# Channel-major down-projection with stationary weights in a GFNet and MLP-mixer kernel: residual on VectorE, 32x32 block transposes, 256-byte stores

## The chip, the core and the metric

The kernel runs on one core of a Trainium2 chip. The time is that of one execution on the device in microseconds (us). TensorE (PE in the profile) multiplies matrices and writes its sums to PSUM banks; PEld is its weight load. VectorE (DVE) and ScalarE (ACT) read PSUM and write SBUF. GpSimd (POOL), SyncE (SP) and ScalarE issue DMAs. Every engine takes its own instructions in program order and waits on semaphores for the others.

## The reference: what is computed

The batch is 8, a sequence has 3008 tokens, a token has 256 channels. All results are float32; the four mixer weights arrive as float64.

```python
X = np.fft.rfft(x, axis=1)                       # x: (8, 3008, 256)
Y = X * (filt_r + 1j * filt_i)[None, :, :]
y = np.fft.irfft(Y, n=3008, axis=1)
...
h = np.maximum(y.transpose(0, 2, 1) @ w_tok1, 0.0) @ w_tok2     # token mixing, 3008 -> 256 -> 3008
u = y + h.transpose(0, 2, 1)
h2 = np.maximum(u @ w_ch1, 0.0) @ w_ch2                         # channel mixing, 256 -> 1536 -> 256
return u + h2
```

## The kernel before

**The filter.** A sequence of 3008 is taken as 64 x 47 points. `a_unit` does the 64-point transforms on TensorE, ScalarE copies them out and stores them to `z_tmp` in HBM. `b_unit` (L344) loads them again, does the 47-point transform and multiplies by the filter in six VectorE instructions (L352 to L357) from the one PSUM bank `b`; `bi_unit` (L360) does the inverse 47-point transform of the product one step later, and ScalarE copies it to SBUF (L366) and stores it to `g_tmp`. The inverse 64-point transform is never done by itself: its matrix `wai` is folded into the token weights (`w1_fold`) and applied again in `u_unit` (L416).

**The mixer.** `mix(b)` handles one sequence. `token_hidden` makes the token hidden layer in 96 matmul instructions (L397). After it the sequence goes by in `MT` = 6 token tiles `m` of 512 tokens, the last of 448. For a tile, `u_unit` writes `ut`, which is u with channels on the partitions: two halves `dh` of 128 channels by 512 tokens. Then there are `JT` = 12 steps `jt` of 128 hidden channels each. `hidden` (L420) has weights `wc1` as the stationary operand and `ut` moving, two matmuls, and ScalarE applies the relu (L426). `down` (L429) comes two steps later and has the hidden activations `hh` as the stationary operand, 128 tokens at a time, and `wc2` (256 columns) moving: four matmuls a step, one for each quarter q of the tile. So the output has tokens on the partitions, in the two banks `po0` and `po1`. In step `jt` = 0 eight matmuls against an identity matrix (L441) first put `ut`, transposed, into the same banks: that is the residual u. The profile counts two matmul instructions and two weight loads for each float32 matmul in the code. After step 11 ScalarE copies `po0` and VectorE `po1` to SBUF (L452 to L455), and GpSimd stores them in four DMAs (L459), each row run 2 KB long (two neighbouring tokens).

**The order of the work** is written out by hand, as the program order of every engine. In step i of `mix` come, in this order: a piece of weight conversion from float64 (`convert`, only at the start of sequence 0); `hidden` of item i; `u_unit` for the next tile at `jt` 5 and 7; one step of the filter of the next group of sequences, given after the `yield`; `down` of item i-2. A tile's last `down` so stands in step 12m + 13 of its sequence. The groups are (0), (1, 2), (3, 4), (5, 6), (7): during sequence 0 a filter step comes in every step i, in sequences 1 to 6 in every step with even i, and in sequence 7 there is none. A group's filter takes 24 steps of `a_unit` for each of its sequences, two empty ones, and 33 of `b_unit` and `bi_unit`.

**Buffers.** The banks `po0`, `po1`, `b`, `i`, `acc` and `a` exist once each, `pg` (of `hidden`) twice. The tile `u` has two buffers, `hh` four, the output tile `o` two. The conversion of the weights (`rounded`, L204 to L212) is one ScalarE and five VectorE instructions per chunk; the chunks of `wc1` and `wc2` that are not needed at once are converted in steps 0 to 9 of sequence 0 (`LAST`).

Of the kernel before, what the change touches and what calls it, by code (L numbers as in the profile page):

```python
# [10 lines left out]
FP32 = mybir.dt.float32  # L11
# [3 lines left out]
ALU = mybir.AluOpType  # L15
# [4 lines left out]
N1 = 47  # L20
N2 = 64
NF = N // 2 + 1
D = 256
P = 128
K2 = 32
A = 24
KR = 4 * A
HALF = 64
# [7 lines left out]
DC = 1536  # L36
JT = DC // P
DH = D // P
MT = 6
NG = 8  # L40
AHEAD = 6
# [3 lines left out]
def _make_tables():  # L45

    n2 = np.arange(N2)
    wa = np.zeros((P, P))
    wai = np.zeros((P, P))
    for h in range(2):
        r = slice(h * 64, h * 64 + 64)
        for k2 in range(K2):
            th = 2 * np.pi * ((n2 * k2) % N2) / N2  # L60
            c, s = np.cos(th), np.sin(th)
            re, im = 4 * k2 + 2 * h, 4 * k2 + 2 * h + 1
            wa[r, re] = c
# [12 lines left out]
    wi = np.zeros((P, K2, KR))  # L76
    for k2 in range(K2):
        for s in range(2 * A):
            if s < A:
                k, sign, q = k2 + 64 * s, 1.0, s  # L80
            else:
                j = s - A + 1
                k, sign, q = 64 * j - (k2 if k2 else 32), -1.0, 32 + s - A
                if j == A and k2:
                    continue
            th = 2 * np.pi * ((n1 * k) % N) / N
            c, sn = np.cos(th), np.sin(th)
            edge = k in (0, NF - 1)
            if edge:
                sn = np.zeros(N1)  # L90
            if k2:
                wb[re, k2, q] = c
                wb[im, k2, q] = sign * sn
                wb[re, k2, HALF + q] = -sn
                wb[im, k2, HALF + q] = sign * c
            else:
                src = re if s < A else im
                wb[src, k2, q] = c
                wb[src, k2, HALF + q] = -sn
                m = 1.0 if edge else 2.0  # L100
                wi[q, k2, src] = m * c
                wi[HALF + q, k2, src] = -m * sn
    wi[:, 1:, :] = wb[:, 1:, :].transpose(2, 1, 0)
    wi /= N
    f = np.float32
    return wa.astype(f), wai.astype(f), wb.astype(f), wi.astype(f), np.eye(P, dtype=f)


@with_exitstack
def kernel(  # L110
# [10 lines left out]
):  # L121
    nc = tc.nc

    wa_np, wai_np, wb_np, wi_np, id_np = _make_tables()
    wa_d = nc.inline_tensor(wa_np, name="wa_t").ap()
    wai_d = nc.inline_tensor(wai_np, name="wai_t").ap()
    wait_d = nc.inline_tensor(np.ascontiguousarray(wai_np.T), name="wait_t").ap()
    wb_d = nc.inline_tensor(wb_np, name="wb_t").ap()
    wi_d = nc.inline_tensor(wi_np, name="wi_t").ap()
    id_d = nc.inline_tensor(id_np, name="id_t").ap()  # L130


    z_d = nc.dram_tensor("z_tmp", (B, K2, KR, D), FP32, kind="Internal").ap()
# [2 lines left out]
    def pool(name, bufs, **kw):  # L136
        return ctx.enter_context(tc.tile_pool(name=name, bufs=bufs, **kw))

    glob = pool("glob", 1)
# [8 lines left out]
    h1p = pool("h1p", 1)  # L148
    up = pool("up", 2)
    hp = pool("hp", 4)  # L150
    op = pool("op", 2)
    psum = pool("psum", 1, space=bass.MemoryType.PSUM)
    psg = pool("psg", 2, space=bass.MemoryType.PSUM)

    def bank(tag):
        return (psg if tag == "pg" else psum).tile([P, 512], FP32, tag=tag, name="ps_" + tag)

    xlast = glob.tile([P, XC, D], FP32, name="xlast")
    wa = glob.tile([P, P], FP32, name="wa")
    wai = glob.tile([P, P], FP32, name="wai")  # L160
    wai_t = glob.tile([P, P], FP32, name="wai_t")
    ident = glob.tile([P, P], FP32, name="ident")
    filt = glob.tile([P, K2, D], FP32, name="filt")
    w1 = glob.tile([P, A, DT], FP32, name="w1")
    w2 = glob.tile([P, TC, N], FP32, name="w2")
# [1 line left out]
    wc2 = glob.tile([P, JT, D], FP32, name="wc2")  # L167
# [86 lines left out]
    def wc1_load(i):  # L254
        c, q = divmod(i, DC // 512)
        st = stage(512)
        nc.gpsimd.dma_start(st, moe_w_ch1[ts(c, P), ts(q, 512)])
        yield
        rounded(st, 512, [(lambda v: v, wc1[:, c, ts(q, 512)])])

    def wc2_load(i):
        st = stage(512)
        nc.gpsimd.dma_start(st.rearrange("p (j d) -> p j d", d=D),
                            moe_w_ch2[ts(i, 2 * P), :].rearrange("(j p) d -> p j d", p=P))
        yield
        rounded(st, 512, [(lambda v: v, wc2[:, 2 * i:2 * i + 2, :].rearrange("p j d -> p (j d)"))])


    LAST = ((wc2_load, 0), (wc1_load, 1), (wc1_load, 4), (wc2_load, 1), (wc1_load, 2), (wc2_load, 2), (wc1_load, 5),
# [50 lines left out]
    def dft(bs):  # L320
# [10 lines left out]
        wbs, wis, t2s, t3s, prods = {}, {}, {}, {}, {}  # L331
# [28 lines left out]
        def bi_unit(k):  # L360
            ps = bank("i").rearrange("p (b d) -> p b d", b=2)[:, 0:nb, :]
            nc.tensor.matmul(ps[0:KR], wis[k // WC][:, k % WC, :], prods.pop(k), start=True, stop=True)  # L362
            c, r = divmod(k, KC)
            if r == 0:
                t3s[c] = t3p.tile([KR, KC, nb, D], FP32, tag="t3", name="t3")
            nc.scalar.copy(out=t3s[c][:, r], in_=ps[0:KR])  # L366
            if r == KC - 1:
                t3 = t3s.pop(c)
                for i, b in enumerate(bs):
                    nc.scalar.dma_start(g_d[b, ts(c, KC)].rearrange("k r d -> r k d"), t3[:, :, i, :])  # L370
# [32 lines left out]
    def width(m):  # L403
        return 512 if m < MT - 1 else 448

# [23 lines left out]
    def down(b, m, jt, hh, ut, po):  # L429
        w = width(m)  # L430
        if jt == 0:
            for i in range(2):
                po.append(bank("po%d" % i).rearrange("p (a d) -> p a d", a=2))
        end = jt == JT - 1

        for q in (0, 1, 3, 2) if end else range(4):
            n = min(P, w - q * P)
            ps = po[q // 2][0:n, q % 2, :]
            if jt == 0:
                for dh in range(DH):  # L440
                    nc.tensor.matmul(ps[:, ts(dh, P)], ut[:, dh, ds(q * P, n)], ident,  # L441
                                     start=(q % 2 == 0 and dh == 0), stop=False)
            nc.tensor.matmul(ps, hh[:, ds(q * P, n)], wc2[:, jt, :], start=False,  # L443
                             stop=(end and q in (1, 2)))
        if end:
            rows = out[b].rearrange("(n2 n1) d -> n2 n1 d", n1=N1)
            for i in range(2):
                o = op.tile([P, 2, D], FP32, tag="o", name="o")
                copy = nc.scalar.copy if i == 0 else nc.vector.tensor_copy
                short = i == 1 and w < 512  # L450
                if short:
                    copy(out=o[:, 0, :], in_=po[i][:, 0, :])  # L452
                    copy(out=o[0:HALF, 1, :], in_=po[i][0:HALF, 1, :])
                else:
                    copy(out=o, in_=po[i])  # L455
                for h in range(2):
                    n = 1 if short and h else 2
                    lo = h * A + 4 * m + 2 * i
                    nc.gpsimd.dma_start(rows[:, lo:lo + n, :], o[h * HALF:(h + 1) * HALF, 0:n, :])  # L459

    def mix(b, next_ready, convert):
        h1 = token_hidden(b)
# [29 lines left out]
    with tc.manual_schedule():  # L492
        nc.sync.dma_start(wa, wa_d)
        nc.vector.memset(xlast[HALF:P, XC - 1, :], 0.0)
        nc.vector.memset(filt, 0.0)
        convert = weights()
        next(convert)
        for i, _ in enumerate(dft(GROUPS[0])):
            if i == 0:
                for t, src in ((wai_t, wait_d), (wai, wai_d), (ident, id_d)):  # L500
                    nc.scalar.dma_start(t, src)
            if i < A // 2:
                next(convert)
            if 0 < i <= A // 2:
                w1_fold(i - 1)
        for c in range(A // TC4):
            t4_load(0, c)
        for _ in range(TC * N2 // NG + DH):
            next(convert)
        for bs, after in zip(GROUPS, GROUPS[1:] + ((),)):  # L510
            todo = dft(after) if after else iter(())
            done = not after
            for b in bs:
                def next_ready():
                    return b != bs[-1] or done

                for i, _ in enumerate(mix(b, next_ready, convert)):
                    if not done and i % len(bs) == 0:
                        done = next(todo, "end") == "end"
            for _ in todo:  # L520
                raise AssertionError("the filter's steps don't fit beside the mixer's")
# [30 lines left out]
```

## Time and profile before

| What | Value |
|---|---|
| Median of 3 runs | 2972.94 us (2971.87 to 2975.9) |
| Profiled execution, its own time | 2976.47 us |
| Span in the profile | 2974.7 us |
| PE busy | 2870.3 us, 96% |
| PEld busy | 1846.6 us, 62% |
| DVE busy | 776.4 us, 26% |
| ACT busy | 538.2 us, 18% |
| POOL busy | 145.1 us, 5% |
| Mean granted TensorE clock | 0.976 |

"Busy" is the time in which at least one instruction of the engine was under way. Matmuls overlap one another, and the end of one is modelled; so the time that a matmul really takes from its successors is read from the distance between the starts of instructions, and not from its busy time. In a row of the timeline the columns are start, busy time, engine, line, operation, tiles and shapes, number of instructions merged, and in brackets the idle time before and what ended it. In a group's row, "128*128 128x256" is the stationary shape and the moving shape. Behind the group's count stand the busy time, the mean of one in ns, and the idle time ahead of it with what ended most of it.

### The profile page before, as it was taken

To read this page: it belongs to the slowest core of one execution; us is meant where nothing else is said; L and a number is where in the kernel's file an instruction comes from. 1 tells how busy PE (TensorE), PEld (TensorE's weight loads), DVE (VectorE), ACT (ScalarE), POOL (GpSimd) and SP (SyncE) were. 2 spreads that over 40 slices of the span, in tenths; PEclk is the share of its full clock that TensorE was granted. 3 is DMA by queue.
4 is the path that set the end of the run, shared out by engine and by line. 5 is a ranking of instruction groups with operands and counts; after the bars stand their busy time and mean duration, and the time that the engine had idled before them with its cause. 6 is when DMAs were issued, how large, how long until landed. Compare 5 with 4: busy or idle time off the path is not lost.

```text
span 2974.7 us, 25841 instructions
## 1 busy us (share of the span) xinstructions
PE 2870.3 (96%) x10456; PEld 1846.6 (62%) x10456; DVE 776.4 (26%) x1330; ACT 538.2 (18%) x941; POOL 145.1 (5%) x275
## 2 busy tenths in 40 slices
PE   4769999999999999999999999999999999999999
PEld 1346655666666666666665666666666666666665
DVE  5983377000033443000014344100133220000000
ACT  3113222112211111112211111111111111111111
POOL 4010000000000000000000000000000000000000
PEclk8579999999999999999999999999999999999999
DMA  9354332212221221102312121202111110000000
GB/s 227 108 189 155 101 90 80 82 59 76 79 68 46 61 59 66 33 28 81 94 51 64 43 60 50 73 14 77 50 53 54 32 50 22 15 14 8 7 15 14
DMA packets 125717, 189.34 MB, mean 64 GB/s; under 512 B 16632, under 2 KB 84728, under 8 KB 125408
## 3 DMA queue, kind: packets, MB, share of 16 engines
q1 hardware_dynamic: 69520, 90.80, 10.2%
q0 software_dynamic: 15200, 46.36, 6.0%
q10 hardware_dynamic: 40880, 50.54, 5.1%
q8 instruction: 83, 1.36, 0.2%
q14 instruction: 34, 0.28, 0.0%
HBM read 112.66 MB, written 74.97 MB: 63 GB/s over the span
## 4 chain that ended last, share of the span: by engine, by line
PE 93%; DVE 4%; DMA 1%; issue 1%; ACT 0%; POOL 0%; ACTq 0%; POOLq 0%; DVEq 0%
PE ps_po L443 34%; PE ps_pg L423 33%; PE ps_acc L411 6%; PE ps_acc L397 5%; PE ps_b L346 3%; PE ps_i L362 3%; PE ps_po L441 3%; PE ps_acc L416 3%; PE ps_a L315 3%; DMA st<-in_moe_w_tok_dram 1%; DMA x<-in_x_dram 1%; DVE p L355 0%; DVE p L356 0%; DVE p L353 0%; DVE p L354 0%
## 5 line engine op out<-in xcount | busy, mean ns | idle before, releaser
L443 PE MATMUL ps_po<-wc,hh 128*128 128x256 f32 (+1 forms) x4608 | 1128.0, 381 | 0.0
L423 PE MATMUL ps_pg<-u,wc 128*128 128x512 f32 (+1 forms) x2304 | 1069.9, 587 | 0.0
L443 PEld LDWEIGHTS ps_po<-wc,hh 128*128 128x128 f32 (+1 forms) x4608 | 836.1, 188 | 311.2 <-issue 231.5
L426 ACT ACTIVATE hh<-ps_pg 128x512 f32<-128x512 f32 (+1 forms) x576 | 338.7, 588 | 1907.1 <-PE ps_pg L423 1800.7
L423 PEld LDWEIGHTS ps_pg<-u,wc 128*128 128x128 f32 x2304 | 430.5, 190 | 327.3 <-issue 296.4
L418 DVE COPY u<-ps_acc 128x512 f32<-128x512 f32 (+1 forms) x96 | 65.3, 680 | 873.0 <-PE ps_acc L416 873.0
L459 POOL DMA_DIRECT2D out_dram<-o x192 | 100.1, 528 | 2625.3 <-ACT o L455 2613.5
L411 PE MATMUL ps_acc<-w,h 128*128 128x512 f32 (+1 forms) x384 | 180.5, 593 | 27.7 <-ACT h L400 21.5
L352 DVE TENSOR_TENSOR p<-ps_b,filt 64x512 f32<-64x512 f32 (+1 forms) x144 | 85.5, 594 | 440.1 <-PE ps_b L346 439.7
L455 DVE COPY o<-ps_po 128x512 f32<-128x512 f32 x40 | 27.7, 692 | 602.4 <-PE ps_po L443 602.3
L362 PE MATMUL ps_i<-p,wi 128*96 128x512 f32 (+1 forms) x320 | 153.6, 565 | 24.4 <-DVE p L357 14.5
L397 PE MATMUL ps_acc<-t,w 128*128 128x256 f32 x768 | 169.6, 383 | 6.8 <-DMA t<-g_tmp 6.8
L397 PEld LDWEIGHTS ps_acc<-t,w 128*128 128x128 f32 x768 | 147.6, 192 | 28.1 <-DMA t<-g_tmp 7.6
L411 PEld LDWEIGHTS ps_acc<-w,h 128*128 128x128 f32 x384 | 72.1, 191 | 115.6 <-issue 81.1
L346 PE MATMUL ps_b<-t,wb 96*128 96x512 f32 (+1 forms) x288 | 134.8, 551 | 2.0 <-issue 2.0
L441 PEld LDWEIGHTS ps_po<-ident,u 128*128 128x128 f32 (+1 forms) x768 | 114.3, 189 | 30.5 <-issue 23.1
L416 PEld LDWEIGHTS ps_acc<-wai,t 128*128 128x128 f32 x768 | 101.7, 193 | 44.8 <-issue 44.8
L366 ACT COPY t<-ps_i 96x512 f32<-96x512 f32 (+1 forms) x160 | 79.3, 496 | 214.4 <-PE ps_i L362 212.2
L441 PE MATMUL ps_po<-ident,u 128*128 128x128 f32 (+1 forms) x768 | 117.0, 275 | 0.0
L362 PEld LDWEIGHTS ps_i<-p,wi 128*96 128x96 f32 x320 | 54.0, 181 | 98.7 <-issue 93.6
L416 PE MATMUL ps_acc<-wai,t 128*128 128x128 f32 (+1 forms) x768 | 101.2, 275 | 0.0
L346 PEld LDWEIGHTS ps_b<-t,wb 96*128 96x128 f32 x288 | 58.7, 207 | 63.2 <-issue 59.5
(53 smaller groups left out, 961.7 us busy)
## 6 DMA issues: line engine op xcount, KB each, us to landing
z_tmp<-t ACTq DMA_DIRECT2D x96, 256.0 KB, 2.5
t<-z_tmp SPq DMA_DIRECT2D x128, 192.0 KB, 3.3
g_tmp<-t ACTq DMA_DIRECT2D x128, 192.0 KB, 3.1
t<-g_tmp SPq DMA_DIRECT2D x48, 512.0 KB, 5.1
out_dram<-o POOLq DMA_DIRECT2D x184, 128.0 KB, 2.5
x<-in_x_dram SPq DMA_DIRECT2D x176, 128.0 KB, 3.4
wb<-wb_t SPq DMA_DIRECT2D x80, 96.0 KB, 2.0
wi<-wi_t SPq DMA_DIRECT2D x80, 96.0 KB, 2.0
```

The source lines that it names most:

```text
L315: nc.tensor.matmul(ps, wa, xs.pop((b, c)).rearrange("p a d -> p (a d)"), start=True, stop=True)
L346: nc.tensor.matmul(ps, wbs[k // WC][:, k % WC, :], t2s[k // KC][:, k % KC], start=True, stop=True)
L352: nc.vector.tensor_tensor(out=p1[re], in0=ps[re], in1=fr, op=ALU.mult)
L362: nc.tensor.matmul(ps[0:KR], wis[k // WC][:, k % WC, :], prods.pop(k), start=True, stop=True)
L397: nc.tensor.matmul(acc[:, t, :], w1[:, a, ts(t, P)], t4[b, a // TC4][:, a % TC4, :], start=(a == 0 and t == 0), stop=(a == A - 1 and t == ...
L411: nc.tensor.matmul(ps[:, 0:w], h1[:, t, ts(dh, P)], w2[:, t, ds(m * 512, w)], start=(t == 0), stop=False)
L416: nc.tensor.matmul(ps[:, ds(q * P, n)], t4[b, c][:, r, ts(dh, P)], wai[:, 0:n], start=False, stop=(q == 3))
L423: nc.tensor.matmul(ps[:, 0:w], wc1[:, c, ts(jt, P)], ut[:, c, 0:w], start=(c == 0), stop=(c == DH - 1))
L426: nc.scalar.activation(out=hh[:, 0:w], in_=ps[:, 0:w], func=AF.Relu)
L441: nc.tensor.matmul(ps[:, ts(dh, P)], ut[:, dh, ds(q * P, n)], ident, start=(q % 2 == 0 and dh == 0), stop=False)
L443: nc.tensor.matmul(ps, hh[:, ds(q * P, n)], wc2[:, jt, :], start=False, stop=(end and q in (1, 2)))
L459: nc.gpsimd.dma_start(rows[:, lo:lo + n, :], o[h * HALF:(h + 1) * HALF, 0:n, :])
```

## The change

- `down` has its operands exchanged: `wc2` is stationary, 128 hidden channels by 128 output channels, and `hh` moves, up to 512 tokens. There are two matmuls a step, one for each half `dh` of the channels, into `po0` and `po1`. The output now has channels on the partitions.
- The identity matrix and its matmuls are gone. After step 11 VectorE adds `po` to `ut` in place, 128x512 for each half.
- VectorE then transposes the sum in blocks of 32x32 into a tile `r` (two buffers). A partition of `r` holds one token of each 32, and for each of them 64 numbers side by side.
- For these 64 numbers to be neighbouring channels of the output, the channels are permuted: partition (g, i) of half `dh` is channel 64 g + 32 dh + i. The permutation is put in where ScalarE copies the filtered data out of PSUM (L366), in the rows of `wc1` (four DMAs per chunk in place of one) and in the columns of `wc2` (two VectorE additions per chunk in place of one).
- The store of a tile is 16 DMAs from GpSimd in place of four: 32 partitions each, runs of 256 bytes.

```diff
 def wc1_load(i):
-        nc.gpsimd.dma_start(st, moe_w_ch1[ts(c, P), ts(q, 512)])
+        for g in range(CB):
+            nc.gpsimd.dma_start(st[ts(g, CW)], moe_w_ch1[ds((g * DH + c) * CW, CW), ts(q, 512)])
...
 def wc2_load(i):
-        rounded(st, 512, [(lambda v: v, wc2[:, 2 * i:2 * i + 2, :].rearrange("p j d -> p (j d)"))])
+        def tile_of(dh):
+            return lambda v: v.rearrange("p (j g e i) -> p e j g i", j=2, e=DH, i=CW)[:, dh]
+
+        rounded(st, 512, [(tile_of(dh), wc2[:, 2 * i:2 * i + 2, ts(dh, P)].rearrange("p j (g i) -> p j g i", i=CW))
+                          for dh in range(DH)])
...
 def bi_unit(k):
-            nc.scalar.copy(out=t3s[c][:, r], in_=ps[0:KR])
+            nc.scalar.copy(out=t3s[c][:, r].rearrange("p b (e g i) -> p b g e i", e=DH, i=CW),
+                           in_=ps[0:KR].rearrange("p b (g e i) -> p b g e i", e=DH, i=CW))
...
 def down(b, m, jt, hh, ut, po):
         w = width(m)
         if jt == 0:
-            for i in range(2):
-                po.append(bank("po%d" % i).rearrange("p (a d) -> p a d", a=2))
+            for dh in range(DH):
+                po.append(bank("po%d" % dh))
         end = jt == JT - 1
-
-        for q in (0, 1, 3, 2) if end else range(4):
-            n = min(P, w - q * P)
-            ps = po[q // 2][0:n, q % 2, :]
-            if jt == 0:
-                for dh in range(DH):
-                    nc.tensor.matmul(ps[:, ts(dh, P)], ut[:, dh, ds(q * P, n)], ident,
-                                     start=(q % 2 == 0 and dh == 0), stop=False)
-            nc.tensor.matmul(ps, hh[:, ds(q * P, n)], wc2[:, jt, :], start=False,
-                             stop=(end and q in (1, 2)))
+        for dh in range(DH):
+            nc.tensor.matmul(po[dh][:, 0:w], wc2[:, jt, ts(dh, P)], hh[:, 0:w], start=(jt == 0), stop=end)
         if end:
-            ...
+            r = rp.tile([P, 512 // CW, DH, CW], FP32, tag="r", name="r")
+            for dh in range(DH):
+                nc.vector.tensor_tensor(out=ut[:, dh, 0:w], in0=po[dh][:, 0:w], in1=ut[:, dh, 0:w], op=ALU.add)
+            for dh in range(DH):
+                nc.vector.transpose(r[:, 0:w // CW, dh, :], ut[:, dh, 0:w].rearrange("p (k i) -> p k i", i=CW))
+            rows = out[b].rearrange("(e i n1) (g c) -> g e i n1 c", e=2, n1=N1, c=DH * CW)
+            blocks = r.rearrange("p (q h e) d i -> p h e q (d i)", h=2, e=2)
+            for h in range(2):
+                n = min(4, (w - h * HALF + HALF) // P)
+                for e in range(2):
+                    for g in range(CB):
+                        nc.gpsimd.dma_start(rows[g, e, :, ds(h * A + 4 * m, n)], blocks[ts(g, CW), h, e, 0:n])
```

Here `CW` is 32 and `CB` is 4. The constant and the load of the identity are removed as well, and the pool `op` of the output tiles becomes `rp`.

More of the change, by code (lines that the diff above doesn't have):

```diff
@@ L38 @@
 DH = D // P
+CW = 32
+CB = P // CW
 MT = 6
@@ L105, in _make_tables @@
     f = np.float32
-    return wa.astype(f), wai.astype(f), wb.astype(f), wi.astype(f), np.eye(P, dtype=f)
+    return wa.astype(f), wai.astype(f), wb.astype(f), wi.astype(f)
 @with_exitstack
@@ L122 @@
     nc = tc.nc
-    wa_np, wai_np, wb_np, wi_np, id_np = _make_tables()
+    wa_np, wai_np, wb_np, wi_np = _make_tables()
     wa_d = nc.inline_tensor(wa_np, name="wa_t").ap()
@@ L129 @@
     wi_d = nc.inline_tensor(wi_np, name="wi_t").ap()
-    id_d = nc.inline_tensor(id_np, name="id_t").ap()
     z_d = nc.dram_tensor("z_tmp", (B, K2, KR, D), FP32, kind="Internal").ap()
@@ L150 @@
     hp = pool("hp", 4)
-    op = pool("op", 2)
+    rp = pool("rp", 2)
     psum = pool("psum", 1, space=bass.MemoryType.PSUM)
@@ L161 @@
     wai_t = glob.tile([P, P], FP32, name="wai_t")
-    ident = glob.tile([P, P], FP32, name="ident")
     filt = glob.tile([P, K2, D], FP32, name="filt")
@@ L445, in down @@
-        if end:
[L446 to L459, printed above, removed]
+        for dh in range(DH):
+            nc.tensor.matmul(po[dh][:, 0:w], wc2[:, jt, ts(dh, P)], hh[:, 0:w], start=(jt == 0), stop=end)
@@ L499 @@
             if i == 0:
-                for t, src in ((wai_t, wait_d), (wai, wai_d), (ident, id_d)):
+                for t, src in ((wai_t, wait_d), (wai, wai_d)):
                     nc.scalar.dma_start(t, src)
```

## The prediction

> **What bounds the kernel now.** I read the page first: busy shares, slices, chain of waits.
>
> ```profile
> span 2974.7 us, 25841 instructions
> ...
> PE 2870.3 (96%) x10456; PEld 1846.6 (62%) x10456; DVE 776.4 (26%) x1330; ACT 538.2 (18%) x941; POOL 145.1 (5%) x275
> PE   4769999999999999999999999999999999999999
> PEclk8579999999999999999999999999999999999999
> PE 93%; DVE 4%; DMA 1%; issue 1%; ACT 0%; POOL 0%; ACTq 0%; POOLq 0%; DVEq 0%
> ```
>
> PE holds 93% of the chain, and only in the first three of 40 slices (about 223 us) is it short of work. After that every us that TensorE is spared counts, and every new wait of TensorE counts as well. The groups of the edited lines come next.
>
> ```profile
> L443 PE MATMUL ps_po<-wc,hh 128*128 128x256 f32 (+1 forms) x4608 | 1128.0, 381 | 0.0
> L423 PE MATMUL ps_pg<-u,wc 128*128 128x512 f32 (+1 forms) x2304 | 1069.9, 587 | 0.0
> L441 PE MATMUL ps_po<-ident,u 128*128 128x128 f32 (+1 forms) x768 | 117.0, 275 | 0.0
> ```
>
> The new `down` would have the count and shapes of L423, so these rows suggest a gain of 1128.0 + 117.0 - 1069.9 = 175.1 us. I don't take that: overlapping matmuls are counted with their tails, and 381 ns for 256 columns beside 587 for 512 can't be what each takes from the next. I take distances between starts, from the timeline of sequence 7, where nothing else runs.
>
> ```profile
> 2874.28 1.89 PE L443 MATMUL ps_po<-wc,hh 128*128 128x256 f32 x8
> 2876.00 1.88 PE L423 MATMUL ps_pg<-u,wc 128*128 128x512 f32 x4
> 2877.72 1.89 PE L443 MATMUL ps_po<-wc,hh 128*128 128x256 f32 x8
> ...
> 2881.16 0.61 PE L441 MATMUL ps_po<-ident,u 128*128 128x128 f32 x4
> ...
> 2884.68 1.88 PE L423 MATMUL ps_pg<-u,wc 128*128 128x512 f32 x4
> ```
>
> From 2874.28 to 2876.00 the eight 256-column instructions take 1.72; from 2876.00 to 2877.72 four of 512 columns take 1.72 as well. TensorE is paid by column here, weight loads hidden in both. So **in the five full tiles of a sequence exchanging the operands gives nothing**. Step 0 of a tile lasts 2884.68 - 2881.16 = 3.52: the identity costs 3.52 - 1.72 = 1.80.
>
> The tile of 448 tokens is another matter.
>
> ```profile
> 2923.69 1.67 PE L423 MATMUL ps_pg<-u,wc 128*128 128x448 f32 x4
> ...
> 2925.19 1.89 PE L443 MATMUL ps_po<-wc,hh 128*128 128x256 f32 x8
> ...
> 2928.42 0.61 PE L441 MATMUL ps_po<-ident,u 128*128 128x128 f32 x4
> ...
> 2932.16 1.77 PE L423 MATMUL ps_pg<-u,wc 128*128 128x448 f32 x4
> ...
> 2933.77 2.03 PE L443 MATMUL ps_po<-wc,hh 128*128 128x256 f32 x8
> ...
> 2935.74 1.77 PE L423 MATMUL ps_pg<-u,wc 128*128 128x448 f32 x4
> ```
>
> Ahead of this tile's own `down`, four instructions of 448 columns take 2925.19 - 2923.69 = 1.50. The old `down` takes 2935.74 - 2933.77 = 1.97 (the last quarter has 64 tokens as weights and still moves 256 columns), and the `hidden` behind it 2933.77 - 2932.16 = 1.61: 0.11 more than 1.50, as the first weights after a 64-wide load are late.
>
> **The change part by part.** Identity: 1.80 in 40 full tiles, and 2932.16 - 2928.42 - 1.97 = 1.77 in 8 short ones: 72.0 + 14.2 = **86.2 us less**.
>
> Short tile: the new `down` is two matmuls (four instructions) of 448 columns with full weights, hence 1.50. In steps 0 to 8 it saves 0.47 itself and 0.11 in the `hidden` behind it: 9 x 0.58 = 5.2. The last three stand without a `hidden` between:
>
> ```profile
> 2962.34 6.37 PE L443 MATMUL ps_po<-wc,hh 128*128 128x256 f32 x24
> ...
> 2968.75 0.42 DVE L452 COPY o<-ps_po 128x256 f32<-128x256 f32 x1 [40.94 <-PE ps_po L443]
> 2969.09 0.41 DVE L453 COPY o<-ps_po 64x256 f32<-64x256 f32 x1
> 2969.79 1.04 POOL L459 DMA_DIRECT2D out_dram<-o  x2 [0.33 <-DVE o L453]
> ```
>
> Busy 6.37, less about 0.4 of tail, is 6.0 against 3 x 1.50: 1.5. Together 6.7 a sequence, by 8: **53.6 us less**. On TensorE that is -139.8.
>
> The VectorE instructions need prices. The trace has no transpose and no addition of PSUM to SBUF on 128 partitions.
>
> ```profile
> L352 DVE TENSOR_TENSOR p<-ps_b,filt 64x512 f32<-64x512 f32 x96 | 65.5, 683 | 294.2 <-PE ps_b L346 294.2
> L205 DVE TENSOR_SCALAR top<-top 128x512 uint32<-128x512 uint32 x24 | 10.6, 440 | 38.5 <-ACT top L204 38.5
> L212 DVE TENSOR_TENSOR w<-top,rest 128x368 f32<-128x368 f32 x16 | 12.7, 792 | 0.5
> L459 POOL DMA_DIRECT2D out_dram<-o x192 | 100.1, 528 | 2625.3 <-ACT o L455 2613.5 <-issue 5.8 <-DVE o L455 3.2
> L263 POOL DMA_DIRECT2D st<-in_moe_w_ch_dram x6 | 4.3, 719 | 30.7 <-issue 22.9 <-ACT t L317 7.8
> L257 POOL DMA_DIRECT2D st<-in_moe_w_ch_dram x6 | 3.4, 574 | 8.7 <-issue 8.7
> ```
>
> Addition: 0.69, as L352 (PSUM and SBUF in, 512 elements, 683 ns). Transpose of 512 elements: not below 0.44 (L205, the fastest 512 here), not above 1.10 (L212, scattered reading, 792 ns for 368, scaled to 512). I take 0.69, as it streams dense runs like most 512-element rows. [...]
>
> So a tile end asks VectorE for 2 x 0.69 + 2 x 0.69 + gaps, 2.9 us, where one copy of 0.69 stood; ScalarE loses its copy. Does TensorE wait? Queued behind the four instructions is the next filter chain, on which `bi_unit` waits. Sequence 0, a tile end with a filter step:
>
> ```profile
> 405.99 0.68 DVE L352 TENSOR_TENSOR p<-ps_b,filt 64x512 f32<-64x512 f32 x1 [0.91 <-PE ps_b L346]
> ...
> 409.55 0.69 DVE L357 TENSOR_TENSOR p<-p,p 64x512 f32<-64x512 f32 x1
> 410.09 1.02 PE L346 MATMUL ps_b<-t,wb 96*128 96x512 f32 x2
> 410.27 0.69 DVE L455 COPY o<-ps_po 128x512 f32<-128x512 f32 x1
> 410.95 1.02 PE L362 MATMUL ps_i<-p,wi 128*96 128x512 f32 x2
> 411.15 0.68 DVE L352 TENSOR_TENSOR p<-ps_b,filt 64x512 f32<-64x512 f32 x1 [0.19 <-PE ps_b L346]
> ```
>
> A chain without a copy has 0.91 idle before it, with the copy 0.19: about 0.9 fits in. The chain ends at 409.55 + 0.69 = 410.24, L362 takes its product at 410.95: 0.7 more to spare. So 2.9 - 0.9 - 0.7 = 1.3 us of waiting (0.8 to 2.1 with the bounds of the transpose). The banks aren't late: the additions end near 410.24 + 1.4 = 411.7, and `po` is written again at about 411.8 (after `hidden`, L346, L362). From the order of work this happens where a filter step with a chain and a tile end share a step: the chains run in steps 26 to 58 of sequence 0, tile ends are in steps 13, 25, 37, 49, 61; so twice: **2.6 us more** (1.6 to 4.2). In sequences 1 to 6 chains start in even steps and tile ends are odd. There the chain (six instructions, 406.0 to 410.24, 4.2 us) has two `down` and a `hidden` of 1.72 each to finish in, and the next starts only after another `hidden` and L346, some 2.6 after the tile's last matmul; the first addition starts when `po0` is done, 0.9 before that: 2.9 fits into 3.5. Nothing there.
>
> The banks in sequence 7: from the last `down` to the next one lies a `hidden`, 1.72; the second addition ends about 0.9 after the last matmul. Nothing. At a sequence's end the 96 matmuls of L397 follow.
>
> Stores: 16 issues a tile, 0.53 (L459, 64 runs) to 0.72 us each (L263, 256 runs); I take 0.574 (L257, 128 runs as here): 9.2 us a tile, while a tile lasts 12 x 3.44 = 41. `r` has two buffers, so a transpose waits only for stores two tiles back. Hidden, except behind the last tile. **Tail:** now from the last matmul (2968.7) to the end of the span (2974.7) 6.0, of it 2974.7 - 2970.83 = 3.9 behind the last issue. New: second addition 0.62, two transposes 1.3, semaphores 0.5, 16 x 0.574 = 9.2, then 3.9: 15.5. **9.5 us more** (8 with the lower rows, 13 with the upper).
>
> Conversion: a `wc2` chunk ends in two additions of 256 elements (0.42 each, as L452 above) in place of one of 512 (0.69), some 0.2 us more, six times. VectorE's idle time covers all but one chunk:
>
> ```profile
> 235.93 0.69 DVE L212 TENSOR_TENSOR wc<-top,rest 128x512 f32<-128x512 f32 x1
> ...
> 237.69 1.89 PE L443 MATMUL ps_po<-wc,hh 128*128 128x256 f32 x8
> ```
>
> Chunk 1 is ready at 236.62 for the third `down` at 237.69: 1.07 to spare, which 1.80 without the identity and 0.2 more work use up: **0.9 us more** (0 if the conversion moves ahead with TensorE). The three extra issues per `wc1` chunk (1.7 us) lie in a GpSimd queue that has no store before the first tile end. ScalarE's permuted copy has the same elements in runs of 32; ScalarE is 18% busy and has 0% of the chain: nothing, and hidden still if each such copy took half as long again.
>
> Sum on the profiled execution's own 2976.5: -139.8 + 2.6 + 9.5 + 0.9 = -126.8, **2849.7**. The median lies 3.5 below that execution, so 2846 to 2850; I say **2848**. Its own range is 2838 to 2859: 0.01 of misreading in each of 576 `down` is 6, the tail gives -2 to +4, the waits -2 to +2.
>
> **The rivals.**
>
> *Wider matmuls are cheaper by themselves* (the group rows hold): 2976.5 - 175.1 + 13.0 = 2814. For it speaks only the mean duration; the equal 1.72 speaks against. 5%.
>
> *VectorE's wait at every tile end:* if transposes come at the upper bound, or each instruction has more wait ahead of it than I count, all 48 tile ends cost 1.3 to 2.1 more: 62 to 101, hence 2910 to 2950. Against it: chains and tile ends share a step twice only, and DVE is 26% busy. 8%; half of it would be some of the tile ends, 2860 to 2880, 5% beside.
>
> *Slower: the stores don't drain within a tile.* The place is the 16 DMA engines; a tile is 512 KB in 256-byte runs, 2048 packets, 128 an engine.
>
> ```profile
> q1 hardware_dynamic: 69520, 90.80, 10.2%
> q0 software_dynamic: 15200, 46.36, 6.0%
> DMA  9354332212221221102312121202111110000000
> ```
>
> A packet costs 0.102 x 16 x 2974.7 / 69520 = 0.070 us in q1 (1306 bytes) and 0.188 in q0 (3050 bytes): 9 to 24 us a tile, beside loads that take 10 to 30% of the engines: it fits into 41. It would decide above 41/128 = 0.32 us a packet: then both `r` are full, the transpose waits, the additions of the next tile behind it, and `po` stays taken. At 0.47, 128 x 0.47 = 60 us a tile, 48 tiles, 2888, and the 223 us ahead: 3110, slower than before. No packet here costs that, yet the trace has no 256-byte data packet. 5%. [...]
>
> **How the numbers follow.** The forecast 77%; VectorE's waits 8%, and partly 5%; the wide matmul 5%; stores 5%. For 8 in 10 I take 2834 to 2876, which holds the forecast's own range and the partial waits. A change below 0.2% (6 us) can't be told from none. All cases but the stores' are faster: faster 0.94, same 0.01, slower 0.05.
>
> **What the profile after would show.** `down` in a full tile still 1.72 from start to start, also in step 0; 1.50 in the short tile, the `hidden` behind it 1.50. Transposes of 0.44 to 1.10. L362 waiting for L357 about 1.3 us at two tile ends of sequence 0 and nowhere else. A q0 of some 99000 more packets under 512 bytes at less than 0.2 us each, issues near 0.57, the last one about 3.9 ahead of the end. The forecast is wrong if PE idles at tile ends of sequences 1 to 7, if 512-column instructions stand closer than 0.43 apart, or if the transposes wait for stores.

## The result and the profile after

The changed kernel takes 2844.8 us (median of 4 runs, 2843.63 to 2845.49), the kernel before in the same comparison 2972.4: a ratio of 0.9568, 95% interval 0.9552 to 0.9585. The profiled execution took 2844.34 us. Its page, first the totals and the chain of waits by engine:

```profile
span 2842.5 us, 20444 instructions
...
PE 2727.1 (96%) x7384; PEld 1348.8 (47%) x7384; DVE 864.9 (30%) x1472; ACT 510.3 (18%) x893; POOL 469.7 (17%) x869
...
PE 92%; DVE 5%; DMA 2%; issue 1%; ACT 0%; POOL 0%; SPq 0%; ACTq 0%; DVEq 0%; POOLq 0%
```

TensorE still sets the time. The costliest groups, with `hidden` now in L431, `down` in L444, the store in L458:

```profile
L431 PE MATMUL ps_pg<-u,wc 128*128 128x512 f32 (+1 forms) x2304 | 1062.4, 584 | 0.0
L444 PE MATMUL ps_po<-hh,wc 128*128 128x512 f32 (+1 forms) x2304 | 1060.8, 584 | 0.0
L458 POOL DMA_DIRECT2D out_dram<-r x768 | 415.7, 550 | 2177.6 <-DVE r L451 2072.0
```

L444 and the old L441 and L443 differ by 184 us of busy time, yet the kernel gained 127.6. The busy column would have misled. The distances between starts in sequence 7, around a tile end (step 0 of the next tile begins at 2746.32), and in the short tile:

```profile
2742.89 1.88 PE L444 MATMUL ps_po<-hh,wc 128*128 128x512 f32 x4
2744.60 1.88 PE L431 MATMUL ps_pg<-u,wc 128*128 128x512 f32 x4
2746.32 1.88 PE L444 MATMUL ps_po<-hh,wc 128*128 128x512 f32 x4
2748.04 1.88 PE L431 MATMUL ps_pg<-u,wc 128*128 128x512 f32 x4
...
2811.22 1.67 PE L431 MATMUL ps_pg<-u,wc 128*128 128x448 f32 x4
2812.72 1.67 PE L444 MATMUL ps_po<-hh,wc 128*128 128x448 f32 x4
2814.22 1.67 PE L431 MATMUL ps_pg<-u,wc 128*128 128x448 f32 x4
```

`down` is 1.72 in a full tile, in step 0 too, with no gap for VectorE's additions; in the short tile `down` and `hidden` are both 1.50.

Where the time went can be read from the chain in order of time: the first `hidden` of all, and the 96 matmuls with which each of the sequences 1 to 7 begins. The kernel before:

```profile
219.54 1.91 PE ps_pg L423 x4
581.56 20.73 PE ps_acc L397 x96
934.20 20.73 PE ps_acc L397 x96
...
2654.73 20.73 PE ps_acc L397 x96
2962.51 6.22 PE ps_po L443 x24
```

And the changed kernel:

```profile
216.77 1.91 PE ps_pg L431 x4
562.90 20.73 PE ps_acc L405 x96
897.44 20.73 PE ps_acc L405 x96
...
2527.52 20.73 PE ps_acc L405 x96
2818.90 4.52 PE ps_po L444 x12
```

| Stage | before, us | after, us | difference |
|---|---|---|---|
| start to the first `hidden` | 219.54 | 216.77 | -2.8 |
| rest of sequence 0 | 362.02 | 346.13 | -15.9 |
| sequences 1 to 6 | 2073.17 | 1964.62 | -108.6 (18.09 each) |
| sequence 7 to its last matmul | 314.00 | 295.90 | -18.1 |
| last matmul to the end of the span | 5.97 | 19.08 | +13.1 |

The sum is -132.2; the two profiled executions differ by 132.1. So seven sequences gain the same 18.1 us (each alone 18.09 or 18.10), sequence 0 lacks 2.2 of it, and the end gives 13.1 back. What lies at the end, VectorE and GpSimd in the timeline:

```profile
2822.69 1.38 DVE L449 TENSOR_TENSOR u<-ps_po,u 128x448 f32<-128x448 f32 x2 [30.42 <-PE ps_po L444]
2823.99 1.16 DVE L451 STREAM_TRANSPOSE r<-u 128x448 f32<-128x448 f32 x2
2825.44 8.64 POOL L458 DMA_DIRECT2D out_dram<-r  x16 [24.21 <-DVE r L451]
```

And GpSimd's own drain at the program's end, from the view by source line (shortest, median and longest of three in ns, first and last start):

```profile
L546 POOLq DRAIN  x3: 46/98/9328, 2832.3 to 2842.2; - x3
```

The last issue ends at 2834.1, but the long drain, which must be the first of the three, runs from 2832.3 to 2841.6: 7.5 us beyond the last issue that the timeline shows. In the kernel before it ended 2.9 us behind the last of four stores (2973.7 and 2970.8). What GpSimd does in its drain isn't shown. The DMA view of the stretch from 2822 to 2843 (40 slices of half a us) has the data landed by then:

```profile
DMA  0000000022222222211122222000000000000000
...
DMA packets 512, 0.46 MB, mean 22 GB/s; under 512 B 256, under 2 KB 384, under 8 KB 512
```

The engines are still from about 2835 on. The second line matters for the prediction: 16 stores with 1792 runs of 256 bytes show 512 packets, and 256 of these are the small ones (16 per store). The data went in 256 packets of some 1.8 KB. In GpSimd's queue a run isn't a packet.

### The profile page after: what moved, and what is told of

It reads as the page before. It is cut to its first block, busy times and chain, and to the rows that moved or that the text cites. A ratio compares the mean times of both kernels' runs of the same rounds, so it can differ in the third digit from the quotient of the medians.

```text
span 2842.5 us, 20444 instructions
## 1 busy us (share of the span) xinstructions
PE 2727.1 (96%) x7384; PEld 1348.8 (47%) x7384; DVE 864.9 (30%) x1472; ACT 510.3 (18%) x893; POOL 469.7 (17%) x869
## 4 chain that ended last, share of the span: by engine, by line
PE 92%; DVE 5%; DMA 2%; issue 1%; ACT 0%; POOL 0%; SPq 0%; ACTq 0%; DVEq 0%; POOLq 0%
PE ps_pg L431 34%; PE ps_po L444 34%; PE ps_acc L419 6%; PE ps_acc L405 5%; PE ps_b L352 3%; PE ps_i L368 3%; PE ps_acc L424 3%; PE ps_a L321 3%; DVE p L361 1%; DVE p L359 1%; DVE p L360 1%; DVE p L358 1%; DVE p L362 1%; DMA xlast<-in_x_dram 1%; DVE p L363 1%
## 5 line engine op out<-in xcount | busy, mean ns | idle before, releaser
L431 PE MATMUL ps_pg<-u,wc 128*128 128x512 f32 (+1 forms) x2304 | 1062.4, 584 | 0.0
L444 PE MATMUL ps_po<-hh,wc 128*128 128x512 f32 (+1 forms) x2304 | 1060.8, 584 | 0.0
L458 POOL DMA_DIRECT2D out_dram<-r x768 | 415.7, 550 | 2177.6 <-DVE r L451 2072.0
L431 PEld LDWEIGHTS ps_pg<-u,wc 128*128 128x128 f32 x2304 | 436.5, 190 | 531.1 <-issue 524.6
L444 PEld LDWEIGHTS ps_po<-hh,wc 128*128 128x128 f32 x2304 | 431.8, 190 | 487.9 <-issue 478.9
L449 DVE TENSOR_TENSOR u<-ps_po,u 128x512 f32<-128x512 f32 (+1 forms) x96 | 64.9, 679 | 726.6 <-PE ps_po L444 725.7
L368 PE MATMUL ps_i<-p,wi 128*96 128x512 f32 (+1 forms) x320 | 153.8, 566 | 25.0 <-DVE p L363 14.5
L352 PE MATMUL ps_b<-t,wb 96*128 96x512 f32 (+1 forms) x288 | 134.7, 551 | 0.6 <-DVE p L361 0.4
L368 PEld LDWEIGHTS ps_i<-p,wi 128*96 128x96 f32 x320 | 53.8, 181 | 100.2 <-issue 92.0
L321 PE MATMUL ps_a<-x,wa 128*128 128x512 f32 x166 | 88.6, 616 | 8.0 <-DMA x<-in_x_dram 7.9
L363 DVE TENSOR_TENSOR p<-p,p 64x512 f32<-64x512 f32 (+1 forms) x160 | 93.2, 583 | 4.9
L362 DVE TENSOR_TENSOR p<-p,p 64x512 f32<-64x512 f32 (+1 forms) x160 | 92.4, 577 | 5.0
```

The lines of the kernel that those rows point to most:

```text
L321: nc.tensor.matmul(ps, wa, xs.pop((b, c)).rearrange("p a d -> p (a d)"), start=True, stop=True)
L352: nc.tensor.matmul(ps, wbs[k // WC][:, k % WC, :], t2s[k // KC][:, k % KC], start=True, stop=True)
L362: nc.vector.tensor_tensor(out=p1[re], in0=p1[re], in1=p2[re], op=ALU.subtract)
L363: nc.vector.tensor_tensor(out=p1[im], in0=p1[im], in1=p2[im], op=ALU.add)
L431: nc.tensor.matmul(ps[:, 0:w], wc1[:, c, ts(jt, P)], ut[:, c, 0:w], start=(c == 0), stop=(c == DH - 1))
L444: nc.tensor.matmul(po[dh][:, 0:w], wc2[:, jt, ts(dh, P)], hh[:, 0:w], start=(jt == 0), stop=end)
```

## The experiments

The kernel before took 2974.28, 2973.89 and 2973.21 us beside the experiments that follow and 2972.4 beside the changed kernel, so a difference in time to the changed kernel can be off by about 2 us. The lengths of sequences within a trace don't have this spread.

**The identity alone.** The kernel before, without the residual's matmuls.

```diff
-            if jt == 0:
-                for dh in range(DH):
-                    nc.tensor.matmul(ps[:, ts(dh, P)], ut[:, dh, ds(q * P, n)], ident, ...)
-            nc.tensor.matmul(ps, hh[:, ds(q * P, n)], wc2[:, jt, :], start=False, ...)
+            nc.tensor.matmul(ps, hh[:, ds(q * P, n)], wc2[:, jt, :], start=(jt == 0 and q % 2 == 0), ...)
```

> The kernel before with the identity matmuls left out, so its output lacks the residual u; nothing else is changed. By the distances between starts (1.80 us in a full tile, 1.77 in a short one) it is 86.2 us faster than the kernel before, about 2886 us, and the timeline shows step 0 of a tile as long as the other steps (1.72 us). The rival that goes by busy time (L441 has 117.0 us) expects 117 us less, 2855 us.

Measured: 2890.43 us, beside 2974.28 for the kernel before; ratio 0.9717 (0.9701 to 0.9733), 83.9 us less. Its chain in order of time, sequence 1:

```profile
570.77 20.73 PE ps_acc L397 x96
912.70 20.73 PE ps_acc L397 x96
```

341.93 us where the kernel before has 352.64: 10.71 in this sequence against 10.77 expected (5 x 1.80 + 1.77). The 117.0 us of busy time aren't what the identity cost.

**Full weights in the short tile.** The kernel before; its last quarter overlaps the one ahead of it.

```diff
-            n = min(P, w - q * P)
-            ps = po[q // 2][0:n, q % 2, :]
+            n = P
+            at = min(q * P, w - P)
+            ps = po[q // 2][0:n, q % 2, :]
...
-            nc.tensor.matmul(ps, hh[:, ds(q * P, n)], wc2[:, jt, :], ...)
+            nc.tensor.matmul(ps, hh[:, ds(at, n)], wc2[:, jt, :], ...)
...
```

> The kernel before with one edit in the 448-token tile: its last quarter takes tokens 320 to 447, so that 128 and not 64 tokens are the weights (the 64 rows that overlap are not stored), which needs one more store per short tile. As many columns move as before. If the 64-wide weights are what makes the short tile's down 1.97 us long and the hidden behind it 1.61, these come to 1.72 and 1.50, which saves 9 x 0.36 + 3 x 0.27 = 4.0 us a sequence, 32 us in all: about 2940 us. The rival, that the short tile gains only by moving fewer columns, expects no change, 2972 us.

Measured: 2940.54 us, 33.7 less; ratio 0.9888 (0.9873 to 0.9902). The short tile's timeline (here `down` is L444):

```profile
2906.81 1.89 PE L444 MATMUL ps_po<-wc,hh 128*128 128x256 f32 x8
2908.54 1.67 PE L423 MATMUL ps_pg<-u,wc 128*128 128x448 f32 x4
2910.04 1.89 PE L444 MATMUL ps_po<-wc,hh 128*128 128x256 f32 x8
```

1.73 and 1.50, where the kernel before has 1.97 and 1.61. Weights of half the width made TensorE slower, twice a step: in the `down` that has the narrow load and in the `hidden` behind it. By the lengths of the sequences it is 4.1 us in each (sequence 1: 348.54 in place of 352.64), 32.8 in all. It is a gain that the kernel before could have had without the change.

**Half as wide, twice as many.** The changed kernel, moving data in pieces of at most 256 columns.

```diff
-            nc.tensor.matmul(po[dh][:, 0:w], wc2[:, jt, ts(dh, P)], hh[:, 0:w], start=(jt == 0), stop=end)
+            for lo in (0, 256):
+                n = min(256, w - lo)
+                nc.tensor.matmul(po[dh][:, ds(lo, n)], wc2[:, jt, ts(dh, P)], hh[:, ds(lo, n)],
+                                 start=(jt == 0 and lo == 0), stop=(end and lo > 0))
```

> The changed kernel with every down matmul cut in two: 256 moving columns and then the rest (256, or 192 in the short tile), with the same weights loaded again. As many columns as in the changed kernel, but twice the instructions and weight loads. If TensorE is paid by column, a full tile's down grows from 1.717 to 1.725 us (480 times, 4 us) and the short tile's by up to 0.12 (weight loads of 0.19 us against 0.16 for 192 columns; 96 times, up to 11 us): 2849 to 2860 us. If wide matmuls are cheaper by themselves, the busy time of 1128 us for this count in the kernel before comes back against 1060.8 us: 67 us more, about 2912 us.

Measured: 2849.48 us, ratio 0.9581 (0.9567 to 0.9595), 4.7 above the changed kernel's median. The timeline, a full tile and the short one:

```profile
2701.43 1.89 PE L446 MATMUL ps_po<-hh,wc 128*128 128x256 f32 x8
2703.16 1.88 PE L431 MATMUL ps_pg<-u,wc 128*128 128x512 f32 x4
...
2799.90 1.68 PE L446 MATMUL ps_po<-hh,wc 128*128 128x256 f32 x8
2801.41 1.67 PE L431 MATMUL ps_pg<-u,wc 128*128 128x448 f32 x4
```

1.73 against 1.72, and 1.51 against 1.50; doubling instructions and weight loads costs 0.01 us a step. TensorE is paid by column here. The rival that wide matmuls are cheaper by themselves (67 us here) falls.

**Transposes twice.** The changed kernel, with the pair of transposes repeated.

```diff
-            for dh in range(DH):
-                nc.vector.transpose(r[:, 0:w // CW, dh, :], ...)
+            for _ in range(2):
+                for dh in range(DH):
+                    nc.vector.transpose(r[:, 0:w // CW, dh, :], ...)
```

> The changed kernel with the two transposes of each tile done twice (the second pair writes the same values again): 1.37 us more on VectorE at each of the 48 tile ends. If VectorE's work there is hidden except at two tile ends of sequence 0 and at the very end, the time grows by 2 x 1.37 + 1.24, some 4 us: 2849 us. If TensorE waits for VectorE at every tile end, it grows by 48 x 1.37 = 66 us: 2911 us.

Measured: 2849.57 us, ratio 0.958 (0.9566 to 0.9594), 4.8 above the changed kernel. Sequence 1 has its old length (903.27 - 568.72 = 334.55, in the changed kernel 334.54), so all but sequence 0 and the end hide VectorE's work, even doubled. The chain in order of time:

```profile
568.72 20.73 PE ps_acc L405 x96
903.27 20.73 PE ps_acc L405 x96
```

Sequence 0 grew by 4.5 us where 2.7 was expected: by 2.9 at the first of its two tile ends with a chain, by 1.2 at the second, and by 0.4 in the first step with a chain (from the starts of L431). The timeline shows the first tile end. Beneath it are two stretches there and two at the second tile end. Each has its length, TensorE's busy time, busy times of the other engines, the granted clock (0.55 in the second row), and the DMA share with its GB/s:

```profile
410.35 1.10 PE L352 MATMUL ps_b<-t,wb 96*128 96x512 f32 x2 [1.40 <-DVE p L361]
...
412.81 3.41 PE L444 MATMUL ps_po<-hh,wc 128*128 128x512 f32 x4
```

```profile
408.00:412.20 4.20, 2.50 (x6) 0.66 (x5) 4.05 (x7) 0.60 (x1) 1.46 (x3) 1.00 0.46 149
412.20:416.00 3.80, 3.80 (x6) 1.52 (x5) 3.60 (x6) 0.58 (x1) 3.80 (x8) 0.55 0.34 86
478.20:482.00 3.80, 2.40 (x6) 0.68 (x4) 3.68 (x7) 0.60 (x1) 3.31 (x7) 1.00 0.73 231
482.00:486.00 4.00, 3.70 (x9) 1.57 (x9) 3.88 (x6) 0.58 (x1) 4.00 (x8) 1.00 0.38 90
```

TensorE idled 1.7 us in the first stretch, and in the next its clock was granted at 0.55: four instructions that take 1.7 took until 416.06, some 3.2. At the second tile end TensorE idled 1.7 us as well (1.40 and 0.30), and the clock stayed at 1.00. Between starts of L431 the first of these steps took 8.99 us and the second 7.30. So the length of the wait alone doesn't decide whether the clock falls.

**Stores in 32 pieces.** The changed kernel, each store cut in two.

```diff
-                        nc.gpsimd.dma_start(rows[g, e, :, ds(h * A + 4 * m, n)], blocks[ts(g, CW), h, e, 0:n])
+                        for lo in (0, 2):
+                            nn = min(2, n - lo)
+                            nc.gpsimd.dma_start(rows[g, e, :, ds(h * A + 4 * m + lo, nn)],
+                                                blocks[ts(g, CW), h, e, lo:lo + nn])
```

> The changed kernel with each tile's 16 stores cut into 32 of half the size (two tokens of 256 bytes per partition, or one). If stores count only behind the last tile, and GpSimd pays a fixed price for each DMA (first issue at 2825.4, its end at 2841.6 in the changed kernel: 16.2 us for 16, or 1.0 each), the time grows by 16 x 1.0 = 16 us, 2861 us. If only the issues shown count (0.55 each) and the rest of the tail is fixed, it grows by 8.8 us, 2854 us. If a tile's stores no longer drain within the tile, all 48 tiles pay: 32 x 1.0 is still under the 41 us of a tile, so the rival of undrained stores expects TensorE to wait at tile ends, several us each, 3000 us or more.

Measured: 2849.76 us, 5.0 above the changed kernel; ratio 0.9584 (0.957 to 0.9598). All sequences keep their lengths, so undrained stores are out. But the tail grew by 5.2 us only, and neither account of it holds. GpSimd's stores in the timeline, and then its drain by source line:

```profile
2826.90 16.60 POOL L460 DMA_DIRECT2D out_dram<-r  x32 [13.89 <-DVE r L451]
```

```profile
L549 POOLq DRAIN  x3: 51/98/7213, 2841.2 to 2848.9; - x3
```

From the first issue to the end of the drain it is 21.5 us for 32 stores, where 16 took 16.2: 0.67 each against 1.01.

**Half the runs, half the stores.** Two kernels to split that price into a part by store and a part by run. Each leaves out half of the output.

```diff
-                n = min(4, (w - h * HALF + HALF) // P)
+                n = min(2, (w - h * HALF + HALF) // P)
```

> The changed kernel with 16 stores per tile that carry two tokens per partition and not four or three: half the output is not stored. In the last tile GpSimd has 16 DMAs with 1024 runs of 256 bytes in all. From its first issue to the end of its drain it took 16.2 us for 16 DMAs with 1792 runs (the changed kernel) and 21.5 us for 32 DMAs with 1792 runs (stores cut in two). If it pays by DMA and by run, these two give 0.33 us a DMA and 0.0061 a run: 16 x 0.33 + 1024 x 0.0061 = 11.5 us. If by DMA alone, 16.2; if by run alone, 9.3.

```diff
-            for h in range(2):
+            for h in range(1):
```

> The changed kernel with only the first eight stores of each tile (h = 0): half the output is not stored. In the last tile GpSimd has 8 DMAs with 1024 runs. By DMA and by run: 8 x 0.33 + 1024 x 0.0061 = 8.9 us from the first issue to the end of the drain; by DMA alone 8.1; by run alone 9.3. Together with the kernel of 16 stores of half the runs it separates the two: the difference is 8 x 0.33 = 2.6 us by DMA and run, 8.1 by DMA alone, 0 by run alone.

One run of each. From the first issue to the end of the drain 13.0 us for 16 stores of 64 runs (2824.7 to 2837.7), and 7.8 for 8 stores of 128 (2826.1 to 2833.9). The difference, 5.2, is neither 2.6, nor 8.1, nor 0. A price by store alone and one by run alone are both excluded; the sum of the two, fitted from two kernels, misses by 1.5 and 1.1. In the first of the two kernels GpSimd also stands still for 2.5 us behind its sixth issue. How its time is made up stays open. What stands is 0.7 to 1.0 us a store, drain included, where an issue shows 0.52 to 0.55.

**The last stores from other queues.** The changed kernel, the very last tile's stores issued by SyncE and ScalarE.

```diff
+                        final = b == B - 1 and m == MT - 1
+                        queue = (nc.sync, nc.scalar)[g % 2] if final else nc.gpsimd
-                        nc.gpsimd.dma_start(rows[g, e, :, ds(h * A + 4 * m, n)], blocks[ts(g, CW), h, e, 0:n])
+                        queue.dma_start(rows[g, e, :, ds(h * A + 4 * m, n)], blocks[ts(g, CW), h, e, 0:n])
```

> The changed kernel with the 16 stores of the very last tile issued by SyncE and ScalarE in turn; all others as before from GpSimd. In the changed kernel 19.1 us lie between the last matmul and the end of the span. If this is GpSimd's serial work on 16 DMAs, the tail shrinks to 2.1 (additions, transposes) + 8 issues of 0.46 + about 2 of landing + 1 for the end: some 9 us, 10 us less, 2835 us. If the tail is the 256-byte writes themselves, it stays near 19 us and the time near 2845 us.

Measured: 2831.92 us (2830.79 to 2832.16), ratio to the kernel before 0.9522 (0.9506 to 0.9538), 12.9 us under the changed kernel. The tail is 8.0 us (2822.4 to 2830.4) in place of 19.1. SyncE's issues in the timeline, and then the DMA view from 2820 to 2831 (a queue's packets, MB and share of 16 engines):

```profile
2824.14 3.68 SPq L460 DMA_DIRECT2D out_dram<-r  x8
```

```profile
DMA packets 2048, 0.46 MB, mean 42 GB/s; under 512 B 2048, under 2 KB 2048, under 8 KB 2048
...
q1 hardware_dynamic: 1024, 0.23, 10.1%
```

The same bytes in the same runs: so the tail was GpSimd, and not the 256-byte writes. Of the 12.1 us between the two profiled executions the tail is 11.1, and 1.0 lies ahead of the first `hidden`. The long drain is still in this trace, behind the stores of the tile before: it runs from 2798.4 to 2806.5, though these stores' last issue ends at 2800.2. It belongs to GpSimd's stores, not to the end of the program.

**Transposes one step later.** The changed kernel, with the transposes and stores of a tile put behind the next step's filter chain.

```diff
...
+                held = later[:]
+                later.clear()
                 down(b, m, jt, hhs.pop(i - 2), uts[m], pos.setdefault(m, []))   # appends its transposes and stores to later
+                finish(held)
...
```

> The changed kernel with a tile's two transposes and its stores moved one step later in program order, behind the next step's filter chain (at a sequence's end they follow at once). If the 2.2 us that sequence 0 saves less than the other sequences are the wait of bi_unit and b_unit for VectorE at two tile ends, sequence 0 gets some 2 us shorter, the others stay, and the waits of L352 and L368 on VectorE at these two places are gone: 2843 us. If sequence 0 lags for another reason (the conversion of the weights), its length stays.

One run: 2843.69 us, which by itself can't be told from the changed kernel. From the first `hidden` (217.19) to sequence 1 (562.21) it is 345.02 us; read in the same way (216.61 to 562.90) the changed kernel has 346.29. So 1.3 us of the 2.2 go, less than expected, and the wait of L352 for L361 is gone. The steps between starts of L431 show the rest: in the changed kernel the two tile ends with a chain have steps of 6.12 and 6.10 us among others of 5.15; with the transposes moved they have 5.15 and, a step later, 5.28. The remainder is mainly in the first two steps with a chain, 5.44 and 5.53 (5.44 and 5.15 in the changed kernel), in a place that I hadn't listed: moving the transposes saved 0.97 and 0.95 at the tile ends and cost some 0.6 elsewhere.

**Both edits, and the last tile's additions and transposes in turn.**

```diff
...
+            if b == B - 1 and m == MT - 1:
+                for dh in range(DH):
+                    add[dh]()
+                    turn(dh)
+                store()
+                return
...
```

> The changed kernel with both edits together, and in the very last tile the order addition, transpose, addition, transpose, so that the first half is transposed while the second half's matmuls run: 10 us less at the end, 2 us less in sequence 0, 0.6 us less before the last stores: 2832 us. If either edit does nothing by itself, 2835 or 2843 us.

Measured: 2831.0 us (2830.26 to 2831.91), ratio to the kernel before 0.9521 (0.9506 to 0.9535); from the version with the last stores moved alone (2831.92) it can't be told, though its sequence 0 is 1.3 us shorter in the trace (344.87 and 346.14). The new order of the last four VectorE instructions gained nothing: they follow one another without a gap from the first addition on, so their order doesn't shorten them: 2.53 us from the first addition to the first issue, 2.48 with the old order.

## Why the prediction was right, step by step

| Term | forecast, us | measured, us |
|---|---|---|
| identity removed | -86.2 | -83.9 (times), -85.7 (8 x 10.71) |
| short tile | -53.6 | -33.7 (times) or -32.8 (8 x 4.10) by full weights alone; some -21 by fewer columns |
| full tiles, operands exchanged | 0 | some -5 (480 steps of 0.010) |
| waits in sequence 0 | +2.6 | +2.2 |
| conversion | +0.9 | 0 |
| tail | +9.5 | +13.1 |
| start | 0 | -2.8 |
| sum on the profiled execution | -126.8 | -132.1 |

That the sum came within 5.3 us is in part luck: the tail cost 3.6 us more than put, the waits and the conversion 1.3 less, and the full tiles and the start, both put at nothing, gave some 5 and 2.8.

*What a full tile gains.* "Nothing" was right to 0.01 us a step. Reading starts in place of busy time is what kept the forecast off 2814.

*Short tile.* The 21 us come from 1.73 against 1.50 in 12 steps of 8 sequences (some 0.22 each), on top of what full weights give. No run shows the 0.4 us of tail put for the last three `down`; by the rows of the kernel before it is 0.17 (a matmul of 256 columns has 381 ns of busy time and follows the one before it by 1.72 / 8 = 0.215).

*VectorE and ScalarE.* An addition took 691 ns and a transpose 685, as priced. ScalarE's permuted copy takes 582 ns for 96x512 where the plain one took 581, so its runs of 32 cost nothing, as forecast.

```profile
L449 DVE TENSOR_TENSOR u<-ps_po,u 128x512 f32<-128x512 f32 x80 | 55.1, 691 | 573.7 <-PE ps_po L444 573.6
L451 DVE STREAM_TRANSPOSE r<-u 128x512 f32<-128x512 f32 x80 | 51.8, 685 | 0.1
...
L451 DVE STREAM_TRANSPOSE r<-u 128x448 f32<-128x448 f32 x16 | 9.3, 618 | 0.0
```

64 elements more cost 67 ns in a transpose, 1.05 ns each, and 68 ns in an addition (691 for 512 and 623 for 448), 1.06 each. A straight line through the two lengths of each leaves 0.15 us for either instruction apart from its elements, an estimate from these four means.

*Waits in sequence 0.* Of the place forecast, a tile end in the changed kernel:

```profile
402.07 1.29 DVE L449 TENSOR_TENSOR u<-ps_po,u 128x512 f32<-128x512 f32 x2
...
403.27 1.29 DVE L451 STREAM_TRANSPOSE r<-u 128x512 f32<-128x512 f32 x2
...
404.49 0.64 DVE L358 TENSOR_TENSOR p<-ps_b,filt 64x512 f32<-64x512 f32 x1
...
407.41 1.10 PE L352 MATMUL ps_b<-t,wb 96*128 96x512 f32 x2 [0.22 <-DVE p L361]
...
408.80 1.07 PE L368 MATMUL ps_i<-p,wi 128*96 128x512 f32 x2 [0.29 <-issue]
```

The four instructions and the late chain are there, twice and not elsewhere, at 0.97 and 0.95 us and not 1.3. TensorE waits first at a place that the forecast hadn't named: L352 may not overwrite the bank `b` before L361 has read it; the wait of L368, which the view puts down to issue, is what is left after that (L363 ends at 408.70, 0.1 before it starts). A third loss of 0.29 is in the first chain step, where no `bi_unit` gives VectorE time.

*Conversion.* The step "1.07 to spare, which 1.80 and 0.2 use up" failed: no step there grew; from the third on all have 4.29 or 4.30 us (6.90 with `u_unit`). The bracket "0 if the conversion moves ahead with TensorE" was the one to take.

*Tail.* The mis-sized term. The issues were cheaper than put (0.54 against 0.574); additions, transposes and semaphores took 2.0 from the last matmul to the first issue, where 2.4 was put (the 0.5 for semaphores came from no row). But "then 3.9" behind the last issue was 8.4. I had carried over what followed four stores of 64 runs; GpSimd's drain ends 7.5 us behind the last of 16 and ended 2.9 behind the last of 4.

*Start.* Not forecast. The first `hidden` starts between 218.1 and 219.4 in the three kernels with the old `down`, and between 214.9 (both edits) and 218.1 (32 stores) in the nine with the new one. The latest of these are as late as full weights alone. The nine differ from one another only in work behind that point, yet they are 3.2 us apart, so -2.8 isn't shown to be the change's doing. What sets it isn't settled.

*The stores' rival.* It had 2048 packets a tile at 0.070 to 0.188 us. GpSimd's queue made 256 packets of up to 2 KB, and its share of the DMA engines went from 6.0% to 6.6%:

```profile
q0 software_dynamic: 30976, 46.39, 6.6%
```

"A q0 of some 99000 more packets" was wrong. Where the runs do become packets (SyncE's queue, above), 1024 packets took 10.1% of 16 engines for 11 us, 0.017 us each, a quarter of the lowest price I had. The 2048 packets of SyncE and ScalarE together took 35 us of engine time for 0.46 MB (10.1% and 10.0%); GpSimd's 512 took 34 for the same bytes (10.0% of 16 engines for 21 us). No run shows the 0.47 us a packet with which this rival came to 3110; 0.017 in SyncE's queue and 0.07 in GpSimd's (34 us by 512) stand in its place.

## What to carry to other kernels

On a saturated TensorE, price an edit by the distance between the starts of instructions in the stage concerned: exchanging the operands of a matmul moves the same columns and was worth 0.01 us of 1.72 here, removing columns was worth about those (an identity 1.8 us a tile, a padded last tile 0.22 a step), and weights of half the width cost extra by themselves (0.35 a step). What was moved to VectorE here was free where its next work had slack, and cost 2.2 us where it had none; look for the few steps where two such loads fall together, and for the bank that is freed late as well as for the product that comes late. At the very end nothing hid anything (the tail grew by 13.1 us): count the whole of the last tile's path, the issuing engine's drain included, and try its stores on other queues (12.9 us less here).

## What the runs showed of the hardware that I had not expected

- GpSimd's drain goes on after its stores' data has landed: with 16 stores at the end it lasts until 7.5 us after the last issue and some 6 after the last byte. With the same stores issued by SyncE and ScalarE the tail is 11 us shorter.
- Runs of 256 bytes travel in packets of up to 2 KB from GpSimd's queue (512 packets for the 1792 runs of the last tile, 256 of them small) and one by one from SyncE's and ScalarE's (2048 packets, all under 512 bytes), at 0.017 us each.
- With the transposes doubled, 1.7 us without a matmul were followed by 3.8 us at a mean granted clock of 0.55, in which four instructions took 3.2 us in place of 1.7; 1.7 us at the next tile end with a chain left it at 1.00, and so did 0.5 us at the first one in the changed kernel. What brought the clock down in the one case isn't shown.
- A weight load of 64 columns between loads of 128 costs 0.24 us in its own `down` (1.97 against 1.73) and 0.11 in the `hidden` behind it (1.61 against 1.50), though the load itself shows 135 ns where one of 128 shows 190.
